# A decode attention kernel: each K and V load dealt by partition halves to SyncE's and ScalarE's DMA queues

## The chip, the cores and the metric

The kernel runs on one core of a Trainium2 chip. The metric is device microseconds of one execution, the median over repeated runs, lower is better. The core has five engines with an instruction stream each: TensorE (PE, with its weight loads as PEld), VectorE (DVE), ScalarE (ACT), GpSimd (POOL) and SyncE (SP). Data comes from memory (HBM) through 16 DMA engines. A DMA that SyncE issues stands in one hardware queue (q1 in the profile), one that ScalarE issues in another (q10), and the same 16 DMA engines work for both.

## The reference

Two attention blocks, A and B, of the same shapes, are computed one beside the other and joined in the last dimension. Each is one step of decoding: one query row for each of 2 batch entries and 32 heads, against 8192 cached keys and values of 192 elements. All inputs are bf16.

```python
def block(x, k_cache, v_cache, wq, wo):          # once for A, once for B
    # x (2, 1, 640), k_cache and v_cache (2, 32, 8192, 192), wq (640, 6144), wo (6144, 640)
    q = (x @ wq).reshape(2, 1, 32, 192).transpose(0, 2, 1, 3)
    scores = einsum("bhqd,bhkd->bhqk", q, k_cache) * 192 ** -0.5
    p = softmax(scores)
    o = einsum("bhqk,bhkd->bhqd", p, v_cache)
    return o.transpose(0, 2, 1, 3).reshape(2, 1, 6144) @ wo

out = concatenate([block(A), block(B)], axis=-1)  # (2, 1, 1280)
```

The caches are 805 MB of the 837 MB that the kernel reads.

## The kernel before

**Units.** The work is cut into 64 units `u`: a pair of heads of one batch entry (16 pairs and 2 batch entries in each block). For each unit there is one K tile and one V tile of `[128, 128, 192]` bf16, 6 MB each. Partitions 0 to 63 hold the first head of the pair and partitions 64 to 127 the second. Each partition holds 128 consecutive cache rows, which is 48 KB (49152 bytes) in one run of memory.

**Loads.** `loads` is the order K0, K1, V0, K2, V1, K3, ... The tiles go round three buffers `kv[0..2]`, so load `i` may be issued when the reader of load `i - 3` is done: `done(i - 3)`, which is the last DVE multiply of a K tile (`("m", u, 3)`) or the PV matmuls of a V tile (`("pv", u)`). `sp_kv` makes the DMA or, for the last unit's K and the last two V tiles, several pieces (`KSPLIT`, `VSPLIT`). All are issued by SyncE, in order, at L215 (the helper `dma`). A reader waits until the load's semaphore stands at 16 more for each load of that buffer.

**One unit.** VectorE multiplies the K tile by the broadcast query `qbc`, in four chunks (`dve_mul`, L298, into `prod`). TensorE adds groups of the products by matmuls with the identity (`pe_sum`, L412, into `scps`), and VectorE finishes the sums (`dve_red`, L304) and takes the maximum (L310). GpSimd reduces it over partitions, ScalarE scales it (`act_nb`, L324) and makes the exponentials (`act_exp`, L332). TensorE multiplies them with the V tile (`pe_pv`, 64 matmuls, L435, into `ops`). ScalarE moves the result (`act_f1`, L342), a small matmul normalizes and transposes it (`pe_f3`, L368), and ScalarE stores it (`act_f4`, L352). ScalarE also copies the query of a later unit (`act_a0`, L361).

**Order of the work.** Each engine's program is a `_Stream`, a list of instructions with the keys that they wait for and the keys that they signal. `put(table, slot, order, ...)` places an instruction in the slot of a unit; within a slot the numbers `order` decide. `emit` writes a stream out as straight code. `emit_loop` writes the slots before `FIRST` (3) as straight code, then a hardware loop over ten rounds of six units each, whose semaphore values come from a register, and then the rest as straight code. Before the change SP and POOL use `emit`, and DVE, ACT and PE use `emit_loop`.

**Beginning and end.** SyncE first issues the two `wq` matrices (`wqa` and `wqb` of both blocks: 6 MB into a `kv` buffer and 1.5 MB into a `prod` buffer each), behind them K0 at once, and K1 and V0 when the query projections of block A (`("pj", 0)`) and B (`("pj", 1)`) have read their weights. At the end the two `wo` matrices are loaded into free `kv` buffers, and the two output rows are stored.

Of the kernel before, what the change touches and what calls it, by code (L numbers as in the profile page):

```python
# [87 lines left out]
def build_kernel(nc, blocks, out):  # L88
# [14 lines left out]
    UG = GP * B  # L103
# [5 lines left out]
    NBUF = 3  # L109
# [11 lines left out]
    with ExitStack() as es:  # L121
        sb = lambda name, shape, dt: es.enter_context(nc.sbuf_tensor(name, shape, dt))
        ps = lambda name, shape, dt: es.enter_context(nc.psum_tensor(name, shape, dt))
        sem = lambda name: es.enter_context(nc.semaphore(name))
# [30 lines left out]
        reg = {}  # L155
        S_sp = _Stream("sp", sem("s_sp"), reg)
        S_pe = _Stream("pe", sem("s_pe"), reg)
        S_act = _Stream("act", sem("s_act"), reg)
        S_dve = _Stream("dve", sem("s_dve"), reg)
        S_pool = _Stream("pool", sem("s_pool"), reg)  # L160
        bsem = [sem(f"bsem{i}") for i in range(NBUF)]
# [10 lines left out]
        loads = []  # L172
# [6 lines left out]
        bcount = [0] * NBUF  # L179
        for i, (kind, u) in enumerate(loads):  # L180
            buf[kind, u] = i % NBUF
            cuts = (KSPLIT if kind == "k" else VSPLIT).get(u)
            if cuts is None:
                bcount[i % NBUF] += 1
                reg[(kind, u)] = (bsem[i % NBUF], 16 * bcount[i % NBUF])
            else:
                for c in range(len(cuts) - 1):
                    reg[(kind, u, c)] = (sem(f"{kind}s{u}_{c}"), 16)

        CB = T * Dh // (Hn * Dh)  # L190
        assert CB == DC - 1 and TC * Dh == Hn * Dh
# [11 lines left out]
        def key(name, *idx):  # L203
            for i in idx:
                if i < 0:
                    return None
            return (name,) + tuple(idx)
# [5 lines left out]
        def dma(out_ap, in_ap, k):  # L213
            s = reg[k][0]
            return lambda eng: eng.dma_start(out_ap, in_ap).then_inc(s, 16)  # L215
# [4 lines left out]
        def sp_wq(blk):  # L220
            src = blocks[blk]["wq"].rearrange("(j c) n -> j (c n)", c=DC)
            n = CB * Hn * Dh
            return [dma(kv[1 + blk][:].rearrange("p t d -> p (t d)"), src[:, :n], ("wqa", blk)),
                    dma(prod[blk][:].rearrange("p t d -> p (t d)"), src[:, n:], ("wqb", blk))]
# [13 lines left out]
            src = blocks[blk]["wo"].rearrange("(p i) n -> p (i n)", i=WI)  # L238
            return dma(wo_i(blk, i0, i1 - i0), src[:, i0 * D:i1 * D], ("wo", blk, n))

        def sp_kv(kind, u):
            hp, b = u // B, u % B
            blk, h = hp // PPB, 2 * (hp % PPB)
            src = blocks[blk][kind][b, h:h + 2].rearrange("s (p t) d -> (s p) t d", p=64)
            t = kv[buf[kind, u]]
            cuts = (KSPLIT if kind == "k" else VSPLIT).get(u)
            if cuts is None:
                return [dma(t[:], src, (kind, u))]
            return [dma(t[:, t0:t1, :], src[:, t0:t1, :], (kind, u, c))
                    for c, (t0, t1) in enumerate(zip(cuts[:-1], cuts[1:]))]  # L250

        NX = NBLK * B
# [7 lines left out]
        def q_bank(hp):  # L260
            tiles = ([scps[0], scps[1], ops[0], ops[1], ops[2], oTps], [outps, scps[0], scps[1], ops[0], ops[1], ops[2]])
            return tiles[hp // PPB][hp // GP - (hp // PPB) * (PPB // GP)]

        def pe_proj(hp, c):
            blk = hp // PPB
            src = kv[1 + blk] if c < CB else prod[blk]
            o = (c if c < CB else 0) * Hn * Dh + (hp % PPB) * QW
            r = 32 * (hp % GP)
            return lambda eng: eng.matmul(q_bank(hp)[r:r + 32, 0:QW], xpad[:, blk, c, :],  # L269
                                          src[:].rearrange("p t d -> p (t d)")[:, o:o + QW],  # L270
                                          start=(c == 0), stop=(c == DC - 1))

        def q_rows(blk):
            out = []
            for g in range(NG):
                hps = [hp for hp in range(GP * g, min(GP * g + GP, NP)) if hp // PPB == blk]
                if hps:
                    r0, r1 = 32 * (hps[0] % GP), 32 * (hps[-1] % GP) + 32
                    rows = [(r0, r1)] if r0 == 0 else [(r, r + 32) for r in range(r0, r1, 32)]
                    out += [(hps[-1], g, slice(*r)) for r in rows]  # L280
            return out

        def act_q(hp, g, r):
            return lambda eng: eng.activation(q_sb[r, g, :], q_bank(hp)[r, 0:QW], ACTF.Identity)

        def dve_q(hp, g, r):
            return lambda eng: eng.tensor_copy(q_sb[r, g, :], q_bank(hp)[r, 0:QW])  # L287
# [69 lines left out]
        def act_a0(u):  # L357
            def fn(eng):
                for s in range(2):
                    r = slice(64 * s, 64 * s + 64)  # L360
                    ins = eng.activation(qbc[u % NQ][r, :], qps[r, s * Dh:(s + 1) * Dh], ACTF.Identity)  # L361
                return ins
            return fn, ("a0", u % NQ)
# [33 lines left out]
        def pe_q(u):  # L397
            hp, b = u // B, u % B
            col = 32 * (hp % GP) + b

            def fn(eng, at):
                g = at(hp // GP, 1)
                mov = q_sb[0:96, hp // GP, :] if isinstance(g, int) else \
                    q_sb[:].rearrange("p g n -> p (g n)")[0:96, bass.ds(g * QW, QW)]
                return eng.matmul(qps[:, 0:QW], ident[0:96, col:col + 1].broadcast_to([96, 128]), mov,  # L405
                                  start=True, stop=True)
            return fn, ("at", "q", hp % GP, b)
# [34 lines left out]
        act_tab = [[] for _ in range(NSLOT)]  # L442
# [3 lines left out]
        def put(tab, slot, order, fn, waits, sig):  # L446
            tab[slot].append((order, len(tab[slot]), fn, waits, sig))

        FIRST, TIMES = 3, 10
# [29 lines left out]
        def done(i):  # L479
            if i < 0:  # L480
                return None
            kind, u = loads[i]
            return ("m", u, NCH - 1) if kind == "k" else ("pv", u)

        for k in range(NBLK):
            for fn in sp_wq(k):
                S_sp.add(fn)
        for i, (kind, u) in enumerate(loads):
            for n, fn in enumerate(sp_kv(kind, u)):
                S_sp.add(fn, waits=[done(i - NBUF) if i >= NBUF else ("pj", i - 1) if i else None] if n == 0 else [])  # L490
        for k in range(NBLK):
            for n in range(len(WCUT[k]) - 1):
                w = ("pv", LASTU) if WCUT[k][n] >= WMAIN[k] else (("m", LASTU, NCH - 1), ("pv", LASTU - 1))[k]
# [6 lines left out]
                   waits=[("id0",)], sig=("id1",))  # L500
# [11 lines left out]
        for a in range(2):  # L512
            S_dve.add((lambda r: (lambda eng: eng.tensor_copy(sel[r, :], ident[r, r])))(slice(32 * a, 32 * a + 2)),
                      waits=[("id1",), ("sel0",)], sig=("sel",) if a == 1 else None)
# [2 lines left out]
            S_act.add(sp_x(blk))  # L517
        S_act.add(lambda eng: eng.memzero(actd[:, 0:1]), sig=("actd",))
        S_act.add(lambda eng: eng.activation(actd[:, 1:2], actd[:, 0:1], ACTF.Exp), waits=[("actd",)])
        for k in range(NBLK):  # L520
            hps = range(PPB * k, PPB * k + PPB)
            for c in range(DC):
                for hp in hps:
                    w = [("xp",), ("wqa", k) if c < CB else ("wqb", k)] if hp == hps[0] else []
                    S_pe.add(pe_proj(hp, c), waits=w + ([("qev", 0), ("qevd", 0)] if k and c == 0 and hp == hps[0] else []),
                             sig=None if c < DC - 1 else ("pj", k) if hp == hps[-1] else ("pjh", hp))
            rows = q_rows(k)
            for n, (hp, g, r) in enumerate(rows):
                w = [("pj", k) if hp == hps[-1] else ("pjh", hp)] + ([("q0",)] if g == NG - 1 else [])
                if k == 0 and n % 2 == 0:  # L530
                    S_dve.add(dve_q(hp, g, r), waits=w, sig=("qevd", 0) if n == len(rows) - 2 else None)
                else:
                    S_act.add(act_q(hp, g, r), waits=w, sig=("qev", k) if n == len(rows) - 1 else None)
            if k == 0:
                for u in range(B):
                    S_pe.add(pe_q(u)[0], waits=[("qev", 0), ("qevd", 0), ("id1",), key("a0", u - 1)], sig=("pq", u), tag=pe_q(u)[1])
                    S_act.add(act_a0(u)[0], waits=[("pq", u)], sig=("a0", u))

        for tab, S in ((dve_tab, S_dve), (act_tab, S_act), (pe_tab, S_pe), (pool_tab, S_pool)):
            for slot in range(NSLOT):  # L540
                for _, _, fn, waits, sig in sorted(tab[slot], key=lambda e: (e[0], e[1])):
                    fn, tag = fn if isinstance(fn, tuple) else (fn, None)
# [15 lines left out]
        for half in range(2):  # L558
            S_act.add((lambda h: lambda eng: eng.activation(y_out(0, h), y_ps(0, h), ACTF.Identity))(half),
                      waits=[("y", 0, half)], sig=("oev", 0, half), slot=E)  # L560
# [5 lines left out]
        with nc.Block() as block:  # L566
            @block.sync
            def _(eng):
                S_sp.emit(eng)

            @block.gpsimd
            def _(eng):
                S_pool.emit(eng)

            @block.vector
            def _(eng):
                S_dve.emit_loop(eng, FIRST, UG, TIMES)

            @block.scalar
            def _(eng):  # L580
                S_act.emit_loop(eng, FIRST, UG, TIMES)

            @block.tensor
            def _(eng):
                S_pe.emit_loop(eng, FIRST, UG, TIMES)
# [49 lines left out]
```

## Time and profile before

| what | value |
|---|---|
| median of 3 runs | 1945.47 us (1945.41 to 1946.12) |
| the profiled execution | 1946.29 us, span 1944.5 us |
| what lies around the span | 1.79 us |
| granted TensorE clock, mean | 0.943 of full |
| busy: PE, PEld, DVE, ACT, POOL | 80%, 39%, 55%, 12%, 3% of the span |
| moved | 837.00 MB, 430 GB/s over the span |

"Busy" is the share of the span in which an engine had an instruction running. The DMA row of the profile is the mean busy share of the 16 DMA engines, and a queue's share is the time that its packets took on 16 engines. The trace holds one record for each packet, the piece that one DMA engine moves at once: here one partition's run of 49152 bytes, and a packet of 4 bytes that counts up the semaphore behind each DMA's data. "To landing" is the time from the issue of a DMA to its last byte's signal.

### The profile page before, as it was taken

What the parts mean: (1) busy time and instruction counts of PE and PEld (TensorE: products, weight loads), DVE (VectorE), ACT (ScalarE), POOL (GpSimd) and SP (SyncE); (2) the same over time, 40 slices, a digit from 0 to 9 for tenths busy, and PEclk for the clock granted to TensorE, in tenths of its full rate; (3) what the DMA queues carried; (4) which work ended last, traced back from release to release, by engine and by line L of the source; (5) the groups of instructions that cost most, each with busy time, mean ns of one, the idle gap of its engine ahead of it and who ended that gap; (6) DMA issues with size and microseconds to landing.
All of it is one profiled execution on the core that took longest, in us unless ns stands there. A gap on an engine that the chain in (4) does not pass through costs nothing.

```text
span 1944.5 us, 19551 instructions
## 1 busy us (share of the span) xinstructions
PE 1547.3 (80%) x7862; PEld 757.9 (39%) x7862; DVE 1068.0 (55%) x778; ACT 237.0 (12%) x788; POOL 58.6 (3%) x143
## 2 busy tenths in 40 slices
PE   3587888888877878878878888877877877887889
PEld 1243434434434434434434434433433433433445
DVE  1665565565565565565565565565465565565560
ACT  1011111111111111111111111111111111101110
POOL 0000000000000000000000000000000000000000
PEclk8899989989999999999988988999999999999999
DMA  9999999999999999999999999999999999999998
GB/s 414 432 429 432 434 432 433 430 436 433 432 431 436 433 433 430 437 435 430 430 437 435 431 433 433 434 433 433 432 435 432 434 431 435 433 433 431 435 424 369
DMA packets 21488, 837.00 MB, mean 430 GB/s; under 512 B 2392, under 2 KB 2400, under 8 KB 3040
## 3 DMA queue, kind: packets, MB, share of 16 engines
q1 hardware_dynamic: 21460, 836.78, 99.8%
q8 instruction: 10, 0.16, 0.0%
q14 instruction: 6, 0.05, 0.0%
q10 hardware_dynamic: 12, 0.01, 0.0%
HBM read 836.77 MB, written 0.01 MB: 430 GB/s over the span
## 4 chain that ended last, share of the span: by engine, by line
DMA 45%; PE 29%; DVE 18%; issue 5%; another core or an unknown queue 2%; SPq 0%; ACT 0%; DVEq 0%; ACTq 0%
DMA kv<-in_B_k_cache_dram 23%; DMA kv<-in_A_k_cache_dram 21%; PE ops L435 19%; DVE prod L298 16%; PE scps L412 10%; DVE sc L304 2%; DMA kv<-in_B_wo_dram 1%; PE ops L388 0%; SPq L215 0%; PE oTps L368 0%; DVEq L83 0%; ACT o_sb L342 0%; ACT oTx L352 0%; PE qps L405 0%
## 5 line engine op out<-in xcount | busy, mean ns | idle before, releaser
L298 DVE TENSOR_TENSOR prod<-kv,qbc 128x6144 bf16<-128x6144 bf16 x256 | 852.8, 3352 | 580.2 <-DMA kv<-in_A_k_cache_dram 218.8
L412 PE MATMUL scps<-prod,ident 128*128 128x512 bf16 x3072 | 786.8, 414 | 362.0 <-DVE prod L298 362.0
L435 PE MATMUL ops<-kv,pb 128*34 128x384 bf16 x4096 | 676.8, 326 | 0.9 <-ACT o_sb L342 0.9
L412 PEld LDWEIGHTS scps<-prod,ident 128*128 128x128 bf16 x3072 | 305.9, 105 | 827.1 <-DVE prod L298 447.6
L435 PEld LDWEIGHTS ops<-kv,pb 128*34 128x34 bf16 x4096 | 395.5, 98 | 284.2 <-issue 26.7
L304 DVE TENSOR_REDUCE sc<-scps 128x32 f32<-128x512 f32 x256 | 176.0, 688 | 213.5 <-PE scps L412 213.5
L324 ACT ACTIVATE nb<-mg 64x1 f32<-64x1 f32 x128 | 25.7, 201 | 1176.7 <-POOL mg L290 1175.9
L332 ACT ACTIVATE pb<-sc,nb 64x128 bf16<-64x128 f32 x128 | 109.9, 858 | 4.0
L290 POOL PARTITION_ALL_REDUCE mg<-mp x64 | 25.9, 405 | 1673.9 <-DVE mp L310 1673.9
L352 ACT ACTIVATE oTx<-oTps 96x4 f32 (+1 forms) x128 | 18.2, 180 | 446.5 <-PE oTps L368 446.5
L332 ACT ACTIVATION_READ_ACCUMULATOR pb<-sc,nb 64x1 f32 x128 | 62.4, 487 | 0.0
L361 ACT ACTIVATE qbc<-qps 64x192 bf16<-64x192 f32 x130 | 42.3, 325 | 3.3 <-PE qps L405 1.0
L342 ACT ACTIVATE o_sb<-ops 2x192 f32<-2x192 f32 x128 | 40.0, 313 | 7.1 <-PE ops L435 6.3
L310 DVE TENSOR_REDUCE mp<-sc 64x1 f32<-64x128 f32 x128 | 35.9, 280 | 4.0
L368 PEld LDWEIGHTS oTps<-rc,o_sb 34*96 34x96 f32 x256 | 26.3, 160 | 20.9 <-issue 20.0
L293 POOL PARTITION_ALL_REDUCE lall<-rs x64 | 28.9, 452 | 149.5 <-ACT pb L332 149.5
L368 PE MATMUL oTps<-rc,o_sb 34*96 34x2 f32 x256 | 31.8, 226 | 0.8 <-ACT o_sb L342 0.8
L405 PE MATMUL qps<-q_sb,ident 96*128 (+1 forms) x65 | 21.9, 336 | 1.7 <-DVE q_sb L287 0.9
L563 DVE CAST out_sb<-ops 2x320 bf16<-2x320 f32 x1 | 0.5, 479 | 29.7 <-PE ops L388 29.7
L388 PE MATMUL scps<-kv,oT 128*2 128x320 bf16 x96 | 14.9, 321 | 0.0
L388 PE MATMUL ops<-kv,oT 128*2 128x320 bf16 x96 | 14.0, 299 | 0.8 <-DMA kv<-in_B_wo_dram 0.6
L269 PE MATMUL scps<-kv,xpad 128*32 128x384 bf16 x48 | 8.8, 443 | 7.1 <-DMA kv<-in_A_wq_dram 7.1
(56 smaller groups left out, 93.7 us busy)
## 6 DMA issues: line engine op xcount, KB each, us to landing
kv<-in_A_k_cache_dram SPq DMA_DIRECT2D x32, 6144.0 KB, 29.1
kv<-in_A_v_cache_dram SPq DMA_DIRECT2D x32, 6144.0 KB, 27.9
kv<-in_B_k_cache_dram SPq DMA_DIRECT2D x31, 6144.0 KB, 29.1
kv<-in_B_v_cache_dram SPq DMA_DIRECT2D x30, 6144.0 KB, 27.8
kv<-in_A_wo_dram SPq DMA_DIRECT2D x4, 1920.0 KB, 26.2
kv<-in_A_wq_dram SPq DMA_DIRECT2D x1, 6144.0 KB, 17.7
kv<-in_B_wq_dram SPq DMA_DIRECT2D x1, 6144.0 KB, 36.3
kv<-in_B_k_cache_dram SPq DMA_DIRECT2D x2, 3072.0 KB, 25.3
```

Source lines behind the costliest of these rows:

```text
L290: return lambda eng: eng.partition_all_reduce(mg[u % 2][:], mp[u % 2][:], 128, bass.bass_isa.ReduceOp.max)
L293: return lambda eng: eng.partition_all_reduce(lall[u % 2][:], rs[u % 2][:], 128, bass.bass_isa.ReduceOp.add)
L298: return (lambda eng: eng.tensor_tensor(prod[c % 2][:], t[:, c * TC:(c + 1) * TC, :], q, ALU.mult)), ("m", c, buf["k", u], u % NQ)
L304: return (lambda eng: eng.tensor_reduce(sc[u % 2][:, c * TC:(c + 1) * TC], sc_tile(u, c), AXL.X, ALU.add)), ("r", c, u % 2)
L310: ins = eng.tensor_reduce(mp[u % 2][r, s:s + 1], sc[u % 2][r, :], AXL.X, ALU.max)
L332: ins = eng.activation(pb[u % 2][r, :, 0::2, s::2].rearrange("p b a j -> p b j a"), sc[u % 2][r, :].rearrange("p (b j a) -> p b j a", a=2, ...
L342: ins = eng.activation(o_sb[r, :], ops[u % NO][r, a * Dh:(a + 1) * Dh], ACTF.Identity)
L361: ins = eng.activation(qbc[u % NQ][r, :], qps[r, s * Dh:(s + 1) * Dh], ACTF.Identity)
L368: ins = eng.matmul(oTps[0:96, 2 * h:2 * h + 2], o_sb[:, 96 * h:96 * h + 96], rc[u % 2][:], start=True, stop=True)
L388: return lambda eng: eng.matmul(y_ps(blk, half), oT[:, blk, i, :], wo_i(blk, i)[:, half * NH2:(half + 1) * NH2], start=(i == 0), stop=(i = ...
L412: ins = eng.matmul(sc_tile(u, c), ident[:], prod[c % 2][:, :, j * DG:(j + 1) * DG], start=(j == 0), stop=(j == NJ - 1))
L435: ins = eng.matmul(ops[u % NO][0:MP, 0:QW], pw[:, o:o + MP], vv[:, j, :], start=(j == 0), stop=(j == TJ - 1))
```

## The change

SyncE issues only the half of each K and V load that goes to partitions 0 to 63 (`side` 0); ScalarE issues the half for partitions 64 to 127 (`side` 1) with a DMA of its own, so it stands in ScalarE's queue. Both count up the same semaphore, whose values are therefore 32 for each load instead of 16. The pieces of the last loads are halved in the same way. The `wq`, `wo`, `x` and output transfers are as before.

ScalarE's half of a load waits for the same event as SyncE's (`load_wait`). It stands in ScalarE's program at slot `u - 2`, behind `act_f4` and ahead of `act_f1`, for a K tile, and at the head of slot `u`, ahead of `act_nb`, for a V tile. The first three loads' halves stand among the query projections, and ScalarE's half of K0 waits for `("wqb", 0)`, while SyncE's half of K0 waits for nothing, as before. ScalarE's whole program becomes straight code (`emit`), since these DMAs go to different tensors.

```diff
-                reg[(kind, u)] = (bsem[i % NBUF], 16 * bcount[i % NBUF])
+                reg[(kind, u)] = (bsem[i % NBUF], 32 * bcount[i % NBUF])
...
-                    reg[(kind, u, c)] = (sem(f"{kind}s{u}_{c}"), 16)
+                    reg[(kind, u, c)] = (sem(f"{kind}s{u}_{c}"), 32)
...
-        def sp_kv(kind, u):
+        def load_kv(kind, u, side):
...
+            rows = slice(64 * side, 64 * side + 64)
...
-                return [dma(t[:], src, (kind, u))]
-            return [dma(t[:, t0:t1, :], src[:, t0:t1, :], (kind, u, c))
+                return [dma(t[rows], src[rows], (kind, u))]
+            return [dma(t[rows, t0:t1, :], src[rows, t0:t1, :], (kind, u, c))
...
+        def load_wait(i):
+            return done(i - NBUF) if i >= NBUF else ("pj", i - 1) if i else ("wqb", 0)
...
-            for n, fn in enumerate(sp_kv(kind, u)):
-                S_sp.add(fn, waits=[done(i - NBUF) if i >= NBUF else ("pj", i - 1) if i else None] if n == 0 else [])
+            for n, fn in enumerate(load_kv(kind, u, 0)):
+                S_sp.add(fn, waits=[load_wait(i) if i else None] if n == 0 else [])
+            if i >= NBUF:
+                for n, fn in enumerate(load_kv(kind, u, 1)):
+                    put(act_tab, u - 2 if kind == "k" else u, 1.9 if kind == "k" else -1, fn, [load_wait(i)] if n == 0 else [], None)
...
+        S_act.add(load_kv(*loads[0], 1)[0], waits=[load_wait(0)])
...
+            S_act.add(load_kv(*loads[k + 1], 1)[0], waits=[load_wait(k + 1)])
...
-                S_act.emit_loop(eng, FIRST, UG, TIMES)
+                S_act.emit(eng)
```

## The prediction

> **What bounds it now.** I read the page first, for its DMA row and its queue table:
>
> ```profile
> DMA  9999999999999999999999999999999999999998
> q1 hardware_dynamic: 21460, 836.78, 99.8%
> q8 instruction: 10, 0.16, 0.0%
> q10 hardware_dynamic: 12, 0.01, 0.0%
> ```
>
> The columns are packets, MB, and share of 16 DMA engines' span. SyncE's queue q1 keeps all 16 busy for 99.8% of the span; q10, ScalarE's, has the x rows and one output. So the bytes bound this kernel, and TensorE at 80% and VectorE at 55% wait for them. The trace's packet records say how: a 49152-byte packet takes 1815 to 1824 ns, and the next starts 1812 ns after it, so one engine moves 27.1 B/ns and sixteen 434 GB/s. A load gives each engine eight packets, 14.5 us, and loads do land 14.53 us apart. K and V are 805.3 MB, 1024 such packets for each engine: 1024 x 1.812 = 1855 us of the span.
>
> Next, how far ahead the queue is filled: the issues table and SyncE's own rows in the steady part.
>
> ```profile
> kv<-in_A_k_cache_dram SPq DMA_DIRECT2D x32, 6144.0 KB, 29.1
> kv<-in_A_v_cache_dram SPq DMA_DIRECT2D x32, 6144.0 KB, 27.9
> ```
>
> ```profile
> 972.76 0.33 SPq L215 DMA_DIRECT2D kv<-in_B_k_cache_dram  x1
> 988.74 0.33 SPq L215 DMA_DIRECT2D kv<-in_B_v_cache_dram  x1
> ```
>
> The last column of the table is issue to landing; the timeline's first two columns are start and duration. 28 to 29 us for 14.5 us of work means that at each issue about 13 us of earlier work is still queued. An issue up to 13 us late costs nothing.
>
> Third, ScalarE around those issues:
>
> ```profile
> 973.28 0.29 ACT L352 ACTIVATE oTx<-oTps 96x4 f32 x2 [7.07 <-PE oTps L368]
> 973.46 0.64 ACT L342 ACTIVATE o_sb<-ops 2x192 f32<-2x192 f32 x2
> 974.12 0.66 ACT L361 ACTIVATE qbc<-qps 64x192 bf16<-64x192 f32 x2
> 993.36 0.41 ACT L324 ACTIVATE nb<-mg 64x1 f32<-64x1 f32 x2 [18.57 <-POOL mg L290]
> ```
>
> ScalarE idles 18.6 us before the maximum and 7 us before oTx.
>
> **Part by part.** The sum is against the profiled 1946.29 us, which is 0.82 us above the median.
>
> *ScalarE's issues, 133 of them at about 0.33 us (SyncE's row).* K's half stands behind act_f4 and ahead of act_f1. Its wait, the PV matmuls, ends about 972.7; f4 ends at 973.6. So ScalarE's half goes out 0.8 us after SyncE's (972.76), inside the 13 us. Queued behind it are f1 and a0, 0.33 us later; the next PV waits for f1 but starts at 991.5, 17 us on. V's half waits for the last multiply (988.7) while ScalarE idles until 993.36; only act_nb is behind it, and the issue ends 4 us before that. Nothing new waits: 0. Without those covers it would be 133 x 0.33 = 44 us.
>
> *Semaphore packets.* Each load has two instead of one on each engine; data follows such a packet 5 ns later. 133 x 5 ns = 0.7 us.
>
> *Turning between two queues at every packet.* The trace of before alternates queues only in a few places. At the end, two 1280-byte q10 packets go out between q1's; the 7680-byte packet behind one took 298 ns beside 291 to 295 elsewhere. Near the start, 49152-byte packets behind a q10 packet took 1860 and 2387 ns, not 1815, in the first 9 us, where packets with no such neighbour took over 2100 too. Behind 16 KB of code (q8) the next data packet took 2365 ns. So 0 to 550 ns a packet, 0 to 563 us. I take the end's row, the same pair of queues in a filled pipe: 3 ns, 3 us.
>
> *Straight code.* A code packet of 16384 bytes takes 1.03 us and the data packet behind it 0.55 us more: it sets its DMA engine back 1.5 us, for good, since no engine has a gap. Ten such packets stand in the trace; between 274 and 1877 us, the loops' time, there is none. ScalarE's 64 units written out will fetch more: an estimate of 3 to 6 packets, from its share of the records (1263 of 19551, where nine units' worth is now stored). They moved various engines before, and only the last engine's delay counts: 0 to 9 us, I take 2.
>
> *The beginning.* Before, SyncE's queue carried wq A, wq B, K0, K1 one behind the other:
>
> ```profile
> 2.94 22.59 SPq L215 DMA_DIRECT2D kv<-in_A_k_cache_dram  x2
> 45.17 0.33 SPq L215 DMA_DIRECT2D kv<-in_A_v_cache_dram  x1
> 71.80 0.33 SPq L215 DMA_DIRECT2D kv<-in_A_k_cache_dram  x1
> 91.72 0.33 SPq L215 DMA_DIRECT2D kv<-in_A_v_cache_dram  x1
> ```
>
> Now ScalarE's K0 and K1 halves (issued about 23.6 and 26) alternate with wq B's packets. wq B lands at about 57 instead of 42 (7 large packets of it remain, each with one of ScalarE's between), and K0, whose other half stands behind wq B, after 8 + 7 + 11 more packets, about 65 us instead of 56.2. The chain K0 multiply, K2 issue (71.8), V1 issue (91.7) moves by 9 us. The queue has 13 us at the first of these and 8 at the second (K2 lands at 99.8): 1 us idle, and 1 us from issue to data. 2 us; if the lone half-load moves at half speed, K0 lands at 72 and it is 9 to 12. I take 3.
>
> Sum: 0 + 0.7 + 3 + 2 + 3 = 8.7 us, of which no term is a gain; the end is two queues draining together and stays. But the large term is missing: whether sixteen engines still run at full rate when each load covers half the partitions. Before, each engine has eight rows of all 128. Now a half gives each engine four rows. If two engines meet in one region of the tile's memory, each may get half of it. The only rows: the two x rows of A, adjoining partitions, were written by two engines 2 ns apart and took 53 ns each, as if alone; one of B's x packets took 88 ns beside a data stream, the other 55. Bounds 0 to +1855 us (each packet twice as long). I take 2 us here, because engines out of step with each other (a load's sixteen signals spread over 3.3 us, and one packet is 1.8) would write different halves at the same time. Forecast: 1946.29 - 0.82 + 10.7 = about 1957 us.
>
> **The rivals.**
>
> *The halves collide.* Mechanism: two engines with rows in the same region share its rate while both serve the same queue; both turn to the other queue at nearly the same moment, and stay in step. With lag d between the two, a packet of T takes 2T - d in place of T. Loads need all engines, so the closest pair counts; of eight pairs with lags spread evenly over 0 to T, d = T/9, factor 1.89: 1945 + 0.89 x 1855 = 3600 us; a lag of half a packet gives 2870, none 3800. It decides wherever neither partner pushes the other out of step. For: packet times vary by under 10 ns, so little breaks a step once taken, and an engine that runs dry starts again together with its partner. Against: the 53 ns pair, and a lag that grows at each meeting ends in no meeting at all.
>
> [...]
>
> *Turning costs.* If each change of queue restarts the engine as after a code packet, up to 0.55 us a packet: 1945 + 563 = 2510; at 0.2 us, 2150. For: the code packets. Against: q10's own rows at the end.
>
> *Not slower.* With two queues an engine could open the next packet before the last one ends, saving up to 5 ns of 1812, 1024 times: 1945 - 5 = 1940 us. It decides only if the 1812 ns hold such a gap. For: 49152 bytes at the rate of the fastest packet rows leave a few ns. Against: records overlap by 3 ns already. That ScalarE's DMAs could share q1 is no rival: its x rows stand in q10 now.
>
> **How the numbers follow.** Full rate 0.42 (1947 to 1985, a lower end by leaving out the code and turning terms), collision 0.34 (2300 to 3800), turning 0.19 (1985 to 2510), not slower 0.05. The likeliest is the first: 1957 us. 0.2% is 3.9 us, about what can be told from no change; the full-rate case reaches below 1949.4 with some 0.05. Faster 0.05, same 0.05, slower 0.90. The range leaves out the gain and the edge below 1946 (some 0.06) and the collision above 3650 (0.08).
>
> **What would show it.** Right: q1 and q10 with about 50% each, DMA row at 9 throughout, packets still 1815 to 1825 ns, K and V halves landing 28 us after issue; K0's first multiply at 65 us. Collision: the DMA row still at 9 with GB/s well under 433 and packets up to 3.6 us. Turning: packets of 1.9 to 2.4 us, all alike. Late ScalarE issues: ACTq rows more than 13 us behind SPq's and a DMA row below 9. More than 1985 us would make the forecast wrong in its missing term; under 1946, in the sign.

## The result: 3565 us, 1.82 times the time before

The changed kernel takes 3565.44 us (median of 5, 3517.66 to 3747.19) where the kernel before takes 1945.47 us. The times scatter by 6%, those of before by 0.04%. Two of the five runs are long (3728.24 and 3747.19 us) and are left out of the ratio, which is 1.823 with a 95% interval of 1.818 to 1.829; the profiled execution is one of them, so it is read here for its mechanism and not for its total.

The GB/s row of the page before, and then the page after, the lines that answer to the first fence of the prediction:

```profile
GB/s 414 432 429 432 434 432 433 430 436 433 432 431 436 433 433 430 437 435 430 430 437 435 431 433 433 434 433 433 432 435 432 434 431 435 433 433 431 435 424 369
```

```profile
DMA  9999999999999999999999999999999999999998
GB/s 258 213 216 217 219 222 222 222 223 232 229 243 235 240 242 239 241 230 225 231 223 218 217 216 217 217 214 218 217 215 218 216 220 221 219 221 218 218 222 241
q1 hardware_dynamic: 12948, 434.12, 51.3%
q10 hardware_dynamic: 10652, 402.67, 48.4%
q8 instruction: 10, 0.16, 0.0%
```

The 16 DMA engines are as busy as before (a 9 in nearly every slice), and the two queues share them evenly, as forecast. But the bytes in each microsecond have halved: 213 to 258 GB/s in place of 414 to 437 (369 in the last slice). So a busy DMA row says here that packets are in flight, not that they move at the rate of before. The packet records say the same: a 49152-byte packet takes 3.58 us (median; half of them between 3.49 and 3.65), before 1.82.

ScalarE and SyncE around two issues of the steady part (timeline: start, duration, engine):

```profile
1949.69 0.47 SPq L215 DMA_DIRECT2D kv<-in_B_k_cache_dram  x1
1950.12 0.18 ACT L353 ACTIVATE oTx<-oTps 96x4 bf16<-96x4 f32 x1 [19.53 <-PE oTps L369]
1950.13 0.47 ACTq L215 DMA_DIRECT2D kv<-in_B_k_cache_dram  x1
...
1950.65 0.65 ACT L343 ACTIVATE o_sb<-ops 2x192 f32<-2x192 f32 x2 [0.28 <-issue]
...
1980.80 0.47 SPq L215 DMA_DIRECT2D kv<-in_B_v_cache_dram  x1
1980.81 0.50 ACTq L215 DMA_DIRECT2D kv<-in_B_v_cache_dram  x1
```

ScalarE's half of a K load goes out 0.44 us after SyncE's, that of a V load 0.01 us after. In the steady part the issues are not late, so the loss is not there. (The page's times to landing of the two halves can't be told apart in this kernel, because both halves count up one semaphore.)

### The profile page after: what moved, and what is told of

It is laid out like the page before. It is cut to its first block, busy times and chain, and to the rows that moved or that the text cites. A ratio compares the mean times of both kernels' runs of the same rounds, so it can differ in the third digit from the quotient of the medians.

```text
span 3726.5 us, 19219 instructions
## 1 busy us (share of the span) xinstructions
PE 1737.5 (47%) x7862; PEld 818.3 (22%) x7862; DVE 1069.3 (29%) x778; ACT 240.9 (6%) x788; POOL 55.2 (1%) x143
## 4 chain that ended last, share of the span: by engine, by line
another core or an unknown queue 61%; DVE 18%; PE 14%; issue 4%; DMA 2%; DVEq 0%; SPq 0%; ACT 0%
DVE prod L299 15%; PE scps L413 13%; DVE sc L305 2%; DMA kv<-in_B_v_cache_dram 1%; DMA kv<-in_B_wo_dram 1%; PE ops L436 1%; DVE mp L311 1%; DVE lr L316 0%; DVEq L83 0%; PE ops L389 0%; DVE rc L319 0%; SPq L215 0%; DVEq L80 0%; ACT o_sb L343 0%
## 5 line engine op out<-in xcount | busy, mean ns | idle before, releaser
L413 PE MATMUL scps<-prod,ident 128*128 128x512 bf16 x3072 | 830.6, 432 | 1320.8 <-DVE prod L299 1320.8
L436 PE MATMUL ops<-kv,pb 128*34 128x384 bf16 x4096 | 815.7, 369 | 586.1 <-DMA kv<-in_B_v_cache_dram 305.1
L413 PEld LDWEIGHTS scps<-prod,ident 128*128 128x128 bf16 x3072 | 318.2, 109 | 1817.9 <-DVE prod L299 1399.3
L436 PEld LDWEIGHTS ops<-kv,pb 128*34 128x34 bf16 x4096 | 442.8, 109 | 965.4 <-issue 362.4
L353 ACT ACTIVATE oTx<-oTps 96x4 bf16<-96x4 f32 x128 | 15.4, 175 | 1162.3 <-PE oTps L369 1162.3
L319 DVE TENSOR_TENSOR rc<-sel,lr 34x2 f32<-34x2 f32 x64 | 9.8, 153 | 18.8 <-PE oTps L369 16.6
```

What stands on the lines that cost most here:

```text
L413: ins = eng.matmul(sc_tile(u, c), ident[:], prod[c % 2][:, :, j * DG:(j + 1) * DG], start=(j == 0), stop=(j == NJ - 1))
L436: ins = eng.matmul(ops[u % NO][0:MP, 0:QW], pw[:, o:o + MP], vv[:, j, :], start=(j == 0), stop=(j == TJ - 1))
```

## The experiments

### One queue, and two queues with whole partitions

Three kernels separate the two things that the change does to the transfers: a second queue, and halves of the partitions.

The halves alone. SyncE issues both, ScalarE keeps its loop:

```diff
+            rows = [slice(0, 64), slice(64, 128)]
...
-                return [dma(t[:], src, (kind, u))]
...
+                return [dma(t[r], src[r], (kind, u)) for r in rows]
...
```

> SyncE alone issues both halves of each load, partitions 0 to 63 and then 64 to 127, in its one queue; ScalarE keeps its loop and issues nothing. Collision (two DMA engines with rows of the same half share one region of the tile's memory): all sixteen engines serve the same half at the same time, so every 49152-byte packet takes about 3.6 us and the kernel 1945 + 1855 = about 3800 us (3650 to 3820). Turning (the cost lies in changing between two queues): there is one queue, so about 1946 to 1950 us with packets of 1.82 us.

Measured: 3944.14 us, 2.028 times before (2.024 to 2.031), a little over the expected range. Its page:

```profile
GB/s 285 209 209 208 209 210 210 208 209 209 210 209 210 208 209 208 209 210 211 208 209 208 209 210 209 210 208 209 208 210 208 211 208 209 208 208 210 209 208 277
q1 hardware_dynamic: 23588, 836.78, 100.0%
```

One queue, and the rate is still halved: 208 to 211 GB/s in every slice but the first and the last, where `wq` and `wo` are loaded over all 128 partitions. Packets take 3.84 us (median), 2.1 times 1.82.

The second queue alone, with the same waits and straight code, in two forms. First each load, or each piece `t0` to `t1` of a load, is halved along the cache rows:

```diff
...
-                return [dma(t[rows], src[rows], (kind, u))]
...
+                tm = (t0 + t1) // 2
+                cols = slice(t0, tm) if side == 0 else slice(tm, t1)
+                out.append(dma(t[:, cols, :], src[:, cols, :], (kind, u) if len(cuts) == 2 else (kind, u, c)))
...
```

> The changed kernel with the same two queues, the same waits and straight code, but each load is halved along the cache rows of a partition: both halves cover all 128 partitions, in packets of 24576 bytes. Collision: each DMA engine keeps to its own partitions, packets take about 0.91 us, 1946 to 1965 us. Turning: the changed kernel's packets took about 3.58 us where 1.82 are needed, 1.76 us for each turn; here an engine has 2048 packets and turns at least as often, so 1945 + 1855 = 3800 us or more.

Measured: 1964.16 us, 1.010 times before (1.008 to 1.011). Then SyncE issues whole K loads and ScalarE whole V loads:

> SyncE issues whole K loads and ScalarE whole V loads, all 128 partitions, 49152-byte packets, straight code on ScalarE. Collision: packets of 1.82 us, 1946 to 1960 us; with both queues holding a load, each load takes about twice as long to land and nothing else changes. Turning: a turn at every packet while both queues hold work, up to 1945 + 1024 x 1.76 = 3750 us.

Measured: 1964.03 us, 1.009 (1.008 to 1.011), 4 us above the expected range. A stretch of the steady part (stretch, its length, busy time of the engines, then granted clock, DMA share and GB/s), of the kernel before, of this kernel and of the changed one:

```profile
400.00:1400.00 1000.00, 809.08 (x4024) 393.80 (x4023) 573.73 (x416) 121.56 (x408) 25.74 (x68) 0.95 1.00 433
```

```profile
400.00:1400.00 1000.00, 795.18 (x4036) 392.94 (x4034) 571.64 (x412) 120.92 (x414) 28.75 (x68) 0.94 1.00 432
```

```profile
400.00:1400.00 1000.00, 484.91 (x2157) 228.52 (x2154) 298.98 (x216) 67.11 (x222) 13.59 (x36) 0.75 1.00 230
```

The DMA share is 1.00 in all three, with 433, 432 and 230 GB/s. The packets of the whole-load kernel take 1.818 us (median; 1.820 before), those of the columns kernel 0.916 us for 24576 bytes. So turning between the queues costs a few ns at most, and the loss belongs to the halves of the partitions.

### Where the 64 partitions lie

From the fourth load on, one queue loads only 64 partitions of each tile: either 32 to 95, as here, or 0 to 63 (`slice(0, 64)`). Two theories are set against each other. Of the place: the loss comes with 0 to 63 and not with 32 to 95, whose packets stay at 1.82 us, so that the transfers no longer bound the kernel but TensorE's and VectorE's own work. Its estimate is 1600 to 1750 us, from about 24 us a unit at the beginning of before (matmuls with V from 94.51 and from 118.56 us on). Of the count: any 64 partitions are slow.

```diff
+            r = slice(32, 96) if loads.index((kind, u)) >= NBUF else slice(0, 128)
...
-                return [dma(t[:], src, (kind, u))]
+                return [dma(t[r], src[r], (kind, u))]
...
```

> The kernel before, one queue, but from the fourth load on only partitions 32 to 95 of each tile are loaded; the other 64 partitions keep what the first loads left there. [...] Any 64-partition transfer is slow wherever it lies: packets of about 3.6 us, 14.5 us a load, about 1945 us as before.

> The same, with only partitions 0 to 63 loaded from the fourth load on. Both theories of the place and of the count: packets of 3.6 to 3.85 us as in the kernel of two halves in one queue, 4 x 3.84 = 15.4 us a load, 128 x 15.4 + 90 = about 2050 us for half of the bytes. If the loss needed both halves in flight: packets of 1.82 us and 1600 to 1750 us.

Measured: 1669.26 us for the middle and 2038.56 us for the lower half, both as the theory of the place had it. The same stretch, middle and then lower half:

```profile
400.00:1400.00 1000.00, 894.88 (x4779) 454.67 (x4777) 680.79 (x492) 147.04 (x488) 66.95 (x82) 1.00 0.66 257
```

```profile
400.00:1400.00 1000.00, 792.47 (x3830) 382.16 (x3828) 544.75 (x390) 116.74 (x392) 24.62 (x65) 0.91 1.00 206
```

With the middle 64 partitions the DMA engines are idle a third of the time (share 0.66), and TensorE and VectorE are busy for 89% and 68% of it; the packets have a median of 1.815 us. A fifth of them take over 2.2 us: nearly all of those begin within 2.6 us of a load's issue, on engines that had run dry (had nothing queued), and the packets behind them take 1.82. With partitions 0 to 63, the same bytes, count, queue and code, the engines are busy throughout and packets take 3.84 us. It is not the number of partitions, but where they lie: 1.815 us a packet against 3.84. (The rows read from memory differ between these two as well; the spread and crowded rows below are read from the same place and differ in the destination alone.) What sets the two places apart was not shown.

### Loads in three pieces

> One queue (SyncE) and ScalarE's loop as before; each load is cut into partitions 32 to 95, then 0 to 31, then 96 to 127. [...] If any transfer of fewer than 128 partitions runs at half speed wherever it lies: about 3800 us. Turning: 1946 to 1950 us.

Measured: 4013.77 us (3823.35 to 4167.84). By the place, the author's estimate was 1.82 us for the four packets of the middle piece on each engine and 3.6 for the four of the outer pieces, 21.7 us for a load and 1945 + 128 x 7.2 = 2870 us. It was missed by far. The nearest is the other reading, any smaller transfer at half speed, 3800 us, and the middle rows alone, above, rule that out. By the kernel of the middle rows, a DMA engine's four packets of the middle piece ought to take 1.82 us each. In the profile 7% of all packets took 1.85 us or less, but the median was 3.73 and a twentieth took over 5.3. So most packets of the middle piece must be slow too, as if the outer pieces held them up. In the author's assumption so far, in which two partners share a region and others are left alone, they should not be.

### Is it the lag between two partners?

The prediction's rival let two engines slow each other while both are in one half, and stay in step. Two kernels are to push eight of the sixteen engines out of step, with 8-row transfers ("kicks", a row on each of eight engines) into a scratch tile, one ahead of three loads (`KN` is 8192, rows of 16384 bytes) or ahead of every load from the seventh on (`i >= 6`, rows of 12288 bytes):

```diff
+            if i in (6, 7, 8):
...
+                S_sp.add(dma(kick[0:32:4, :], src[0:8, 0:KN], ("kick", nk[0])),
+                         waits=[load_wait(i)] + ([("kick", nk[0] - 1)] if nk[0] > 1 else []))
...
```

> The changed kernel with three extra transfers, one ahead of SyncE's half of loads 6, 7 and 8: 8 rows of 16384 bytes into a scratch tile, which only eight of the sixteen DMA engines carry, one row each. Each puts those eight 0.6 us or more behind their partners, 1.8 us in all, one packet. If partners keep whatever lag they have: packets fall towards 1.8 to 2.0 us from then on and the time to 1950 to 2500 us. If they fall back into step: no change, 3500 to 3750 us.

> The changed kernel with such a transfer (8 rows of 12288 bytes, 0.45 us alone) ahead of SyncE's half of every load from the seventh on: 122 x 0.45 = 55 us more work for eight engines. If the loss comes from partners being in step and a lag breaks it: 2300 to 3200 us, packets spread between 1.8 and 3.6 us. If the lag does not matter or is lost at once: 3550 to 3850 us.

Measured: 3561.95 us (3494.84 to 3680.98) with three of them, 4032.67 us (ratio 2.075, 2.071 to 2.079) with one ahead of each load. The kicks bring no gain in either, and the second is above its expected range. The profiled execution with three kicks took 3551.63 us, and its packets 3.45 us (median). Whether the eight engines kept their lag can't be read, since the records don't name the engine. But the packet records show that the question was put wrongly. In the changed kernel all sixteen engines run at nearly one pace: at any one moment the durations of the sixteen packets in flight differ by 72 ns (mean standard deviation), while their common mean wanders by 205 ns over time. A lag that belongs to each pair would not give that. (In the kernel with three pieces the packets in flight differ by 388 ns, so the pace is not common everywhere.) The mean of those in flight, by how many of the sixteen came from SyncE's queue:

```
from q1     4      6      8     10     12     14     16
mean ns  3565   3503   3389   3518   3598   3683   3739
```

The pace is best when the two halves are served evenly, but even then a packet takes 1.87 times 1.815 us.

### One crowded region, sixteen engines

So the theory became: when one region is crowded, all engines wait, not just those that write to it. Which partitions make a region, no run shows. To see one crowd without any halves, the kernel before gets 31 extra 8-row transfers of 16384-byte rows, into partitions 0, 4, 8 to 28 (spread, as here) or 0 to 7 (crowded, `kick[0:8, :]`):

```diff
+            if i >= 6 and i % 4 == 2:
...
+                S_sp.add(dma(kick[0:32:4, :], src[0:8, 0:KN], ("kick", nk[0])),
...
```

> The kernel before with 31 extra transfers, one ahead of every fourth load: 8 rows of 16384 bytes into partitions 0, 4, 8 to 28 of a scratch tile, one row on each of eight DMA engines, each in a region of its own. No region is crowded: 31 x 0.61 us = 19 us more for eight engines, about 1965 us, and the 49152-byte packets stay at 1.82 us.

> [...] Partners only (a crowded region delays the engines that write to it): the eight other engines' 49152-byte packets stay at 1.82 us. One pace (a crowded region delays all sixteen engines): their packets in flight at that time are stretched too, 16 or more packets over 2.2 us at each of the 31 places, some 500 in all.

Measured: 1964.56 us spread (ratio 1.010), 2051.65 us crowded (1.055, 1.053 to 1.056). The crowded ones cost (2051.65 - 1964.56) / 31 = 2.8 us more at each place. Both kernels read the same rows, so the destination alone makes the difference. The spread ones took 19.0 us in all, and their packets 0.61 us (median), the rate of an engine by itself (16384 bytes at 27.1 B/ns). One sign did not come: the author's estimate for the crowded packets was 2.4 us or more, four times 0.61, and 31 x 2.4 = 75 us or above in all, 2020 to 2050 us. Their median is 0.98 us, and no run shows the factor of four. What is stretched is the large packets. Between 100 and 1850 us, 7 of the 49152-byte packets took over 2.2 us in before, 87 in the spread kernel and 818 in the crowded one. Of the 87, one overlaps an extra packet in time; of the 818, 541 do, about 19 at each of the 29 places in that stretch. Nearly all of the others begin within 4 us of an issue, most of them just after some engines had run dry, as in the kernel of the middle rows.

At the second place no engine had run dry. There, start after the first extra packet and duration, in us, in the order of start:

```
49152 bytes:   0.10 4.31    0.54 2.92    0.66 3.25    0.97 2.96    0.99 2.97    1.02 2.97    1.24 2.89    1.41 2.86
               1.47 2.85    1.61 3.03    1.70 2.85    1.90 2.85    1.95 2.82    2.59 2.75    2.63 2.33    2.79 2.66
```

From 2.8 to 3.4 us these sixteen are the only packets of that size in flight, so they are on all sixteen engines, and all are stretched by a few small packets that crowd into eight neighbouring partitions. The packets behind them take 1.82 to 2.43 us, and from 7.2 us on 1.82 again. At 28 of the 29 places sixteen stretched packets (over 2.05 us) are in flight at once. Only eight engines carry a row of an extra transfer (2640 packets under 512 bytes, 2392 before: eight semaphore packets for each), so the others wait as well. From the fifth to the 25th place some engines also run dry ahead of the extra packets, so the 2.8 us hold some of that too.

This would account for the missed numbers: in the three-piece kernel the outer pieces hold up the middle one, and in the kernels with kicks the extra writes, which go to the lower half, are one more crowd. That is argued, not shown. What holds all of them up was not tried.

### Straight code

```diff
-                S_act.emit_loop(eng, FIRST, UG, TIMES)
+                S_act.emit(eng)
```

> The kernel before with ScalarE's program as straight code and nothing else. The forecast's term: 0 to 9 us, most likely 2, so 1946 to 1955 us. The two kernels with two queues and whole partitions took 18 us more than before; if the code were most of that, about 1960 us.

Measured: 1947.60 us, ratio 1.0011 (1.0002 to 1.0020), 2.1 us more. Its page has five more packets, of 8192 bytes, in the second code queue than before (11 in place of 6):

```profile
q14 instruction: 11, 0.09, 0.0%
```

## Why the prediction was right and where it was wrong

**The direction was right, the forecast was not.** Slower was given 0.90, and 3565 us lies inside 1946 to 3650, close to what the collision rival priced (3600); the range held because it spanned both cases. The forecast of 1957 us was the other case (its own sum gives 1956.2). The step that failed is the one called the large missing term: "Bounds 0 to +1855 us (each packet twice as long). I take 2 us here, because engines out of step with each other (...) would write different halves at the same time." The whole change measured 1620 us; the kernels with whole partitions leave about 1600 of them to this term. Engines that serve both halves at once, eight and eight, still take 3.39 us a packet. The row taken as the nearest, two x rows of 1280 bytes written in 53 ns each, showed no crowding; rows of 16384 bytes into partitions 0 to 7 do, 2.8 us at each place.

**The rival's mechanism was half right.** Where the partitions lie is the cause: 32 to 95 against 0 to 63 shows it for loads (1.815 us a packet against 3.84), and the spread and crowded rows show it for the destination alone (1964.56 us against 2051.65). That engines share a region fits both, but no run shows the regions, nor the eight pairs of engines in the sum. One queue of halves gave the bound of every packet doubled and a little more (3944 us; "none" of lag was priced at 3800). The account of lags between pairs, from which 1.89 came, did not hold: kicks brought nothing, and in the change the sixteen packets in flight differ by 72 ns. That 1.89 stood near the measured 1.82 is luck and no evidence for it. What the runs show is that one crowd is enough to hold up all engines, 2.33 to 4.31 us a packet at the place above. Whether there is a crowd nearly all the time in the change was not counted, since the records don't name the engine.

**The other terms of the sum** can be read in the whole-partition kernels, which have everything of the change but the halves: 18 us, where 8.7 were forecast. By stages of the profiled executions, in us:

| | before | straight code | columns | whole loads |
|---|---|---|---|---|
| up to the first multiply of the ninth unit | 275.4 | 274.6 | 282.8 | 282.5 |
| from there to that of the 63rd unit | 1569.9 | 1572.1 | 1580.2 | 1574.2 |
| from there to the end of the span | 99.3 | 99.1 | 98.8 | 106.8 |

- ScalarE's issues, 0: right in the steady part, 0.44 and 0.01 us behind SyncE's, against 13 us of queued work. K2's half is an exception: it stands in slot 0, behind `act_nb` and `act_exp` of the first unit, and goes out 5.1 us behind SyncE's in the changed kernel and 8.2 us in the columns kernel:

```profile
82.90 0.33 SPq L215 DMA_DIRECT2D kv<-in_A_k_cache_dram  x1
91.14 0.34 ACTq L215 DMA_DIRECT2D kv<-in_A_k_cache_dram  x1
```

- Turning, 3 us, and the semaphore packets, 0.7: of the right size, turning by luck. The row that its 3 ns were read from shows no cost: the 7680-byte packets of before take 291 to 306 ns, and the one of 298 is among them. In the steady part the kernel of whole loads takes 4.3 us more than before, of which the code is 2.2. The columns kernel, with twice as many packets of half the size and two semaphore packets on each engine for a load, takes 10.3 more. The rival at 0.2 to 0.55 us a packet is out.
- Straight code, 2 us: right, 2.1.
- The beginning, 3 us of 2 to 12: mis-sized, about 7 us in both. The first multiply of K0 moved from 56.2 to 67.5 in the columns kernel (65 forecast), which was foreseen. In that kernel the DMA engines idle 4 us more than before between 50 and 150 us, where the prediction had 1; how much of that is K2's late half was not separated. The lines of the K0 multiply, before and in the columns kernel:

```profile
56.23 6.63 DVE L298 TENSOR_TENSOR prod<-kv,qbc 128x6144 bf16<-128x6144 bf16 x2 [30.27 <-DMA kv<-in_A_k_cache_dram]
```

```profile
67.46 6.63 DVE L300 TENSOR_TENSOR prod<-kv,qbc 128x6144 bf16<-128x6144 bf16 x2 [41.03 <-DMA kv<-in_A_k_cache_dram]
```

- The end, "stays": right in the columns kernel, whose queues hold a share of every load as in the change. In the kernel of whole loads it is 7.5 us longer. There the chain that ended last waits 38.8 us for the last V pieces, which ScalarE issued by 1887.2 us, while A's `wo` is issued into SyncE's queue from 1897.4 us on:

```profile
1887.21 38.76 DMA kv<-in_B_v_cache_dram
```

Before, `wo` stands behind V in the one queue, and those pieces land 24.5 us after their issue (median). That the `wo` loads hold them up is the likely reading, not a shown one.

**What would show it** named the right signs for the collision, a full DMA row with GB/s well under 433 and packets up to 3.6 us. These are what came, though a quarter of the packets took over 3.65.

## What to carry to other kernels

When transfers bound a kernel, ask of any new cut of a load which partitions each piece covers, before asking which queue it stands in: the queue cost 1% here and the partitions 80%. Halves along the cache rows, which keep all 128 partitions in every transfer, took 1964 us, halves of the partitions 3565. A DMA row that is full says nothing of the rate (share 1.00 at 433 and at 230 GB/s here): read the GB/s beside it, and compare one packet's duration with the same packet elsewhere.

## What the hardware showed that was not expected

- Sixty-four partitions were slow or not by where they lie: packets of 1.815 us (median) for 32 to 95, 3.84 us for 0 to 63.
- A crowd held up all sixteen DMA engines: packets of 16 KB into partitions 0 to 7 stretched the 49152-byte packets on all engines to 2.33 to 4.31 us at the place shown, while the crowded packets themselves had a median of 0.98 us.
- The first packet of an engine that had run dry was slow: in the kernel of the middle rows most of those took over 2.2 us, the ones behind them 1.82.
- The change does not repeat well, 3518 to 3747 us in five runs, nor do the three pieces, 3823 to 4168; the halves in one queue stay within 3942 to 3948. Why was not tried.
